# Hash attention and MLP mixer: both halves' scores of a head pair in a row, then both products with v

## The chip, the cores and the metric

One NeuronCore of a Trainium2 chip runs the whole program. The metric is device time in microseconds (us), the median of several executions. Runs of one kernel agree here to about 0.5%. Ratios are the mean time of one kernel's runs over that of the other's of the same rounds, so they are not quite the ratio of the medians.

## The reference, cut to what matters

```python
q_bits = (einsum('bhsd,dk->bhsk', q, proj) > 0)      # 6 hash bits per query, the same for keys
mask   = q_bucket[..., :, None] == k_bucket[..., None, :]
scores = where(mask, 0.125 * q @ k^T, -1e9)          # B=4, H=8, S=768, D=64
attn   = exp(scores - max) / sum
x      = (attn @ v) -> (B, S, 512)
u      = x + (relu(x^T @ w_tok1) @ w_tok2)^T          # then the channel MLP on u
```

The change touches attention only, the first 320 us of the program. Heads go in 16 pairs; a pair's 768 queries go in two halves of 384.

## The kernel before: the parts that matter

All arithmetic is fp32. Scores use two row groups of the TensorE array (64 rows each, one per head), the products with v two column groups (64 columns each), the sums of exponentials and the hash products four column groups of 32. The profile calls these forms 64\*128, 128\*64 and 128\*32. An fp32 matmul shows as two instructions (the 12 matmuls of one product with v as x24 in the lines below).

```python
def product(sc, t, c, start):                   # scores of chunk c (128 keys); bits matmul has t = bits
    for i in range(2):
        rows = slice(D * i, D * i + D)
        nc.tensor.matmul(sc[:, i, :HALF], t[rows, 1, P*c:P*c+P], t[rows, 0, qs], ...)
...
sc = psum.tile([P, 2, 512], F32, tag="sc", bufs=3)
product(sc, qkt, c, True); product(sc, bits, c, False)
e = pool.tile([P, 2, HALF], F32, tag="e", bufs=12)
nc.scalar.activation(e, sc[:, :, :HALF], ACT.Exp, scale=SCALE)
...
def hashes(n):                                  # bits of pair n: matmuls, then
    nc.vector.tensor_scalar(g, ps, 0.0, 0.5, op0=ALU.is_gt, op1=ALU.subtract)
    nc.scalar.mul(g, g, bitscale)
    ...                                         # eight small DMAs g -> bitrows, on the sync queue
def weigh(self):                                # the product with v, into ONE psum bank "acc"
    acc = psum.tile([P, 512], F32, name="acc", tag="acc", bufs=1)[:, :HALF]
    for c, e in enumerate(self.es):
        for i in range(2):
            nc.tensor.matmul(acc[D*i:D*i+D], vn[:, i, c], e[:, i], ...)
    nc.scalar.activation(nums[self.n][:, self.half], acc, ACT.Identity, scale=-1.0, bias=vsum)
...
for n in range(len(pairs)):                     # the loop, cut
    for half in range(2):
        now.scores()
        ...                                     # sums of the pair before, hashes(n + 1): if half == 0
        if before: before.weigh()               # product with v of the HALF before
        ...
        if half == 0: load_v(n + 1)
        before = now
```

So TensorE alternates: scores of one half, product of the half before, and so on.

In the lines below PE is TensorE, PEld its weight loads, DVE VectorE, ACT ScalarE, and SPq the sync engine's queue of DMAs. "num" is ACT's copy of a finished product out of PSUM, where this kernel's matmuls write. newton and divide make the reciprocals of the sums (rec, copied once by ACT) and multiply by them. join and turnover convert weights for the later stages, on VectorE with one square on ACT. A bounce, in every second pair, transposes two finished pairs on VectorE and sends them to DRAM in four DMAs.

## Time and profile before

| | before |
|---|---|
| time | 814.28 us, median of 3 |
| span of the profiled run | 811.9 us, of which attention to 321.69 |
| TensorE busy | 803.6 us (99%) |
| a pair of heads, on TensorE | 19.56 us |
| of it: two stretches of scores / two of products / sums / hash product | 10.09 / 8.04 / 0.67 / 0.76 us |

How to read it: with TensorE busy 99% of the span and the chain of waits made of matmuls, no other engine's share says what the kernel could gain.

### The profile page before, as it was taken

How to read it: one execution, taken by the hardware profiler on the slowest of the kernel's cores; microseconds unless marked ns; L12 is line 12 of the kernel's file. 1: busy time of each engine (PE TensorE's matmuls, PEld its weight loads, DVE VectorE, ACT ScalarE, POOL GpSimd, SP SyncE). 2: the span in 40 equal slices, each digit the busy share in tenths (PEclk: the TensorE clock that was granted, in tenths of full speed). 3: DMA queues.
4: the chain of work that ended last, by engine and by line, in shares of the span. 5: the costliest groups of instructions: out<-in, count | busy, mean ns of one | idle time of the engine just before them, and what ended most of it. 6: DMA issues, size and time to landing. Idle time of an engine off the chain costs nothing.

```text
span 811.9 us, 10567 instructions
## 1 busy us (share of the span) xinstructions
PE 803.6 (99%) x3901; PEld 471.6 (58%) x3901; DVE 664.1 (82%) x869; ACT 423.1 (52%) x675; POOL 42.5 (5%) x69
## 2 busy tenths in 40 slices
PE   9999999999999999999999999999999999999996
PEld 4444444444444444455544448876676886676885
DVE  4889898989898676899575969898669897778985
ACT  5787778788888776111022321236774335775111
POOL 1000000000000000000010110011010012000001
PEclk9999999999999999999999999999999999999999
DMA  4335353547444234562008894499854578730455
GB/s 161 128 137 171 132 174 130 159 133 231 140 130 119 81 81 139 173 214 97 1 0 300 297 349 156 176 274 252 272 136 142 210 231 194 232 118 1 160 178 110
DMA packets 88490, 132.30 MB, mean 163 GB/s; under 512 B 29480, under 2 KB 62704, under 8 KB 86128
## 3 DMA queue, kind: packets, MB, share of 16 engines
q1 hardware_dynamic: 82320, 112.60, 42.4%
q0 software_dynamic: 5552, 18.35, 9.4%
q8 instruction: 33, 0.54, 0.3%
q10 hardware_dynamic: 560, 0.61, 0.2%
q14 instruction: 25, 0.20, 0.1%
HBM read 97.21 MB, written 33.69 MB: 161 GB/s over the span
## 4 chain that ended last, share of the span: by engine, by line
PE 99%; DVE 0%; ACT 0%; issue 0%; ACTq 0%
PE b L709 49%; PE sc L345 20%; PE acc L392 16%; PE t L623 5%; PE t L642 5%; PE sums L416 2%; PE hp L306 1%; PE hw L324 1%; PE idle L454 0%; ACT vt L297 0%; ACT e L352 0%; ACT g L311 0%; DVE second L1128 0%; DVE g L310 0%; DVE bits L326 0%
## 5 line engine op out<-in xcount | busy, mean ns | idle before, releaser
L352 ACT ACTIVATE e<-sc 128x768 f32<-128x768 f32 x192 | 153.1, 811 | 13.4 <-PE sc L345 12.5
L345 PE MATMUL sc<-qk 64*128 64x384 f32 x768 | 158.5, 492 | 0.3 <-ACT e L352 0.3
L709 PE MATMUL b<-R,second 128*128 128x256 f32 (+1 forms) x612 | 150.9, 404 | 0.0
L715 ACT COPY c<-b 128x512 f32<-128x512 f32 (+1 forms) x78 | 37.4, 488 | 187.7 <-PE b L709 174.2
L709 PEld LDWEIGHTS b<-R,second 128*128 128x128 f32 x612 | 116.3, 190 | 31.6 <-issue 17.0
L392 PE MATMUL acc<-e,vn 128*64 128x384 f32 x768 | 130.9, 490 | 0.0
L384 DVE TENSOR_TENSOR esd<-esd,e 128x768 f32<-128x768 f32 x128 | 122.3, 955 | 10.4 <-ACT e L352 0.5
L345 PEld LDWEIGHTS sc<-qk 64*128 64x128 f32 x768 | 66.5, 187 | 55.8 <-issue 45.3
L392 PEld LDWEIGHTS acc<-e,vn 128*64 128x64 f32 x768 | 52.3, 137 | 74.9 <-issue 74.3
L709 PE MATMUL b<-XT,WC 128*128 128x256 f32 (+1 forms) x264 | 82.5, 456 | 0.0
L709 PEld LDWEIGHTS b<-XT,WC 128*128 128x128 f32 x264 | 50.2, 190 | 29.6 <-issue 25.1
L345 PE MATMUL sc<-bits 64*128 64x384 bf16 x384 | 62.9, 323 | 0.2 <-DVE bits L328 0.2
L623 PE MATMUL t<-x,W 128*128 128x512 f32 x96 | 41.8, 593 | 0.0
L642 PE MATMUL t<-W,r 128*128 128x384 f32 x128 | 41.8, 486 | 0.0
L398 ACT ACTIVATE num<-acc,vsum 128x384 f32<-128x384 f32 x32 | 18.6, 581 | 41.6 <-PE acc L392 41.2
L437 ACT COPY rec<-rec 32x384 f32<-32x384 f32 x64 | 32.6, 509 | 12.9 <-DVE rec L431 12.4
L380 DVE SCALAR_TENSOR_TENSOR esd<-e 128x768 f32<-128x768 f32 x32 | 30.5, 954 | 9.3 <-ACT e L352 9.3
L709 PE MATMUL b<-XT,SW 128*128 128x256 f32 (+1 forms) x120 | 34.6, 422 | 0.0
L642 PEld LDWEIGHTS t<-W,r 128*128 128x128 f32 x128 | 24.3, 190 | 17.6 <-issue 1.4
L345 PEld LDWEIGHTS <-bits 64*128 64x128 bf16 x384 | 19.3, 94 | 25.4 <-DVE bits L328 0.8
L709 PE MATMUL b<-TA,WC 128*128 128x512 f32 x72 | 33.8, 592 | 0.0
L709 PE MATMUL b<-TA,SW 128*128 128x512 f32 x72 | 32.9, 592 | 0.0
(176 smaller groups left out, 1052.7 us busy)
## 6 DMA issues: line engine op xcount, KB each, us to landing
second<-left SPq DMA_DIRECT2D x18, 1344.0 KB
raw<-in_moe_w_ch SPq DMA_DIRECT2D x16, 768.0 KB
qk<-in_qk SPq DMA_DIRECT2D x15, 768.0 KB
seen<-in_qk POOLq DMA_DIRECT2D x21, 384.0 KB, 4.2
WC<-hidden_left SPq DMA_DIRECT2D x15, 448.0 KB
vn<-in_v SPq DMA_DIRECT2D x16, 384.0 KB
vt<-in_vT SPq DMA_DIRECT2D x16, 384.0 KB
bounced<-stage SPq DMA_DIRECT2D x32, 192.0 KB
```

Of the source, the lines that this page charges most:

```text
L345: nc.tensor.matmul(sc[:, i, :HALF], t[rows, 1, P * c : P * c + P], t[rows, 0, qs], start=start, stop=not start,)
L352: nc.scalar.activation(e, sc[:, :, :HALF], ACT.Exp, scale=SCALE)
L380: nc.vector.scalar_tensor_tensor(self.d, es[0], NR * EPS, es[1], op0=ALU.add, op1=ALU.add,)
L384: nc.vector.tensor_tensor(self.d, self.d, e, op=ALU.add)
L392: nc.tensor.matmul(acc[D * i : D * i + D], vn[:, i, c], e[:, i], start=(c == 0), stop=(c == NR - 1),)
L398: nc.scalar.activation(nums[self.n][:, self.half], acc, ACT.Identity, scale=-1.0, bias=vsum,)
L416: nc.tensor.matmul(ps[at : at + 32], ones[:, :32], self.halves[h].d[:, i], start=True, stop=True,)
L437: nc.scalar.copy(rec[other : other + 32, h], rec[at : at + 32, h])
L623: nc.tensor.matmul(ps, W1[:, r, P * j : P * j + P], x[:, r], start=(r == 0), stop=(r == NR - 1),)
L642: nc.tensor.matmul(ps[:, :HALF], r1[:, j, P * cb : P * cb + P], W2[:, j, HALF * half : HALF * half + HALF], start=(j == 0), stop=(j == NJ ...
L709: nc.tensor.matmul(ps, left(k), right(k), start=start and k == ks[0], stop=stop and k == ks[-1], skip_group_check=True,)
L715: nc.scalar.copy(c, ps)
```

## The change

Intent: run the scores of both halves (12 chunks), then the sums of the pair before and the next pair's hash product, then both products with v. For this the second half's product takes one of the three score tiles as its accumulator, v is asked for a whole pair ahead, and the hash bits come before the last add of the exponentials' sum on VectorE. The core of the diff (cuts are marked):

```diff
             def weigh(self):
                 _, vn, _, vsum = loaded[self.n]
-                acc = psum.tile([P, 512], F32, name="acc", tag="acc", bufs=1)[:, :HALF]
+                if self.half:
+                    acc = psum.tile([P, 2, 512], F32, name="acc", tag="sc", bufs=3)[:, 0, :HALF]
+                else:
+                    acc = psum.tile([P, 512], F32, name="acc", tag="acc", bufs=1)[:, :HALF]
 ... (add split into add, four or five adds, and add_last; esd gets 4 buffers)
+            halves = [Half(n, half) for half in range(2)]
+            if n:
+                load_v(n + 1)
+            for now in halves:
                 now.scores()
+                now.add()
+                if now.half == 0:
+                    now.add_last()
+            if before:
+                before.sums()
+            if n + 1 < len(pairs):
+                hashes(n + 1)
+            halves[1].add_last()
+            if n == 0:
+                load_v(1)
+            load_qk(n + 2)
+            add_values(n)
+            if before:
+                before.newton()
+            weights.join()
+            halves[0].weigh()
 ... (the last pair is set apart)
+            if before:
+                before.divide()
+            weights.turnover()
+            halves[1].weigh()
+            if n and n % 2 == 0:
+                bounce(pool, n - 2)
 ... (the old loop over halves, all removed)
```

More of the change, by code (lines that the diff above doesn't have):

```diff
@@ L373, in scores, with add, add_last @@
                     first_hashes(0, 1)
-            def add(self, k):
+            def add(self):
                 es = self.es
-                if k == 0:
-                    self.d = pool.tile([P, 2, HALF], F32, name="esd", tag="esd", bufs=3)
-                    nc.vector.scalar_tensor_tensor(
-                        self.d, es[0], NR * EPS, es[1], op0=ALU.add, op1=ALU.add,
-                    )
-                for e in (es[2:4], es[4:])[k]:
+                self.d = pool.tile([P, 2, HALF], F32, name="esd", tag="esd", bufs=4)
+                nc.vector.scalar_tensor_tensor(
+                    self.d, es[0], NR * EPS, es[1], op0=ALU.add, op1=ALU.add,
+                )
+                for e in es[2:-1]:
                     nc.vector.tensor_tensor(self.d, self.d, e, op=ALU.add)
+            def add_last(self):
+                nc.vector.tensor_tensor(self.d, self.d, self.es[-1], op=ALU.add)
             def weigh(self):
                 _, vn, _, vsum = loaded[self.n]
-                acc = psum.tile([P, 512], F32, name="acc", tag="acc", bufs=1)[:, :HALF]
+                if self.half:
+                    acc = psum.tile([P, 2, 512], F32, name="acc", tag="sc", bufs=3)[:, 0, :HALF]
+                else:
+                    acc = psum.tile([P, 512], F32, name="acc", tag="acc", bufs=1)[:, :HALF]
                 for c, e in enumerate(self.es):
@@ L460, in attention @@
         )
-        before, both = None, []
+        before = None
         for n in range(len(pairs)):
-            for half in range(2):
-                now = Half(n, half)
+            halves = [Half(n, half) for half in range(2)]
+            if n:
+                load_v(n + 1)
+            for now in halves:
                 now.scores()
-                if half == n == 0:
-                    hashes(1)
-                if half == 0:
-                    add_values(n)
-                now.add(0)
-                quotients = None
-                if len(both) == 2:
-                    quotients, both = Quotients(both), []
-                    quotients.sums()
-                both.append(now)
-                if half == 0 and 0 < n < len(pairs) - 1:
-                    hashes(n + 1)
-                if half == 0:
-                    load_qk(n + 2)
-                if quotients:
-                    quotients.newton()
-                if half and n and n % 2 == 0:
-                    bounce(pool, n - 2)
-                now.add(1)
-                if half:
-                    weights.turnover()
-                else:
-                    weights.join()
-                if before:
-                    before.weigh()
-                if quotients:
-                    quotients.divide()
-                if half == 0:
-                    load_v(n + 1)
-                if half == 0 and n == 2 * NP:
-                    fetch(0, x0)
-                before = now
@@ L498, in attention @@
-        assert not (weights.fetched or weights.begun or weights.ready)
-        quotients = Quotients(both)
-        quotients.sums()
-        quotients.newton()
-        before.weigh()
-        quotients.divide()
+                now.add()
[8 more added lines that the diff above has]
+                load_v(1)
@@ new lines, in attention @@
+            load_qk(n + 2)
[4 more added lines that the diff above has]
+            halves[0].weigh()
+            if n + 1 == len(pairs):
+                before.divide()
+                before = Quotients(halves)
+                before.sums()
+                before.newton()
+                weights.turnover()
+                halves[1].weigh()
+                break
+            if before:
+                before.divide()
@@ L506, in careful_attention @@
+            weights.turnover()
+            halves[1].weigh()
+            if n and n % 2 == 0:
+                bounce(pool, n - 2)
+            if n == 2 * NP:
+                fetch(0, x0)
+            before = Quotients(halves)
+        assert not (weights.fetched or weights.begun or weights.ready)
+        before.divide()
     def careful_attention(pool, psum):
```

## The prediction

> **What bounds the kernel now.** I read the page first: the busy shares, the chain that ended last, and the slices.
>
> ```profile
> PE 803.6 (99%) x3901; PEld 471.6 (58%) x3901; DVE 664.1 (82%) x869; ACT 423.1 (52%) x675; POOL 42.5 (5%) x69
> ...
> PE 99%; DVE 0%; ACT 0%; issue 0%; ACTq 0%
> PE b L709 49%; PE sc L345 20%; PE acc L392 16%; PE t L623 5%; PE t L642 5%; PE sums L416 2%; PE hp L306 1%; PE hw L324 1%; PE idle L454 0%; ACT vt L297 0%; ACT e L352 0%; ACT g L311 0%; DVE second L1128 0%; DVE g L310 0%; DVE bits L326 0%
> ```
>
> The chain is matmuls nearly from end to end, so TensorE sets the time. The change touches only attention (sc, acc, sums, hp). No wait of another engine is on the path for it to take away: in the table of waits for attention PE waits 0.3 us for ACT and 0.2 us for DVE, once each, both in the first pair. What can still be gained lies inside PE's busy time, so I went to the order of time on PE, one stretch of scores and one of products with v (from 112.76 us):
>
> ```profile
> 112.76 0.92 PE L345 MATMUL sc<-qk 64*128 64x384 f32 x4
> 113.51 0.33 PE L345 MATMUL sc<-bits 64*128 64x384 bf16 x2
> 113.67 0.81 PE L345 MATMUL sc<-qk 64*128 64x384 f32 x4
> ...
> 116.90 0.81 PE L345 MATMUL sc<-qk 64*128 64x384 f32 x4
> 117.54 0.33 PE L345 MATMUL sc<-bits 64*128 64x384 bf16 x2
> 117.80 4.09 PE L392 MATMUL acc<-e,vn 128*64 128x384 f32 x24
> 121.82 0.92 PE L345 MATMUL sc<-qk 64*128 64x384 f32 x4
> ```
>
> Columns: start, duration, engine, line, what. A chunk of scores starts every 0.807 us ((116.90 - 113.67)/4), but the first takes 0.91 (112.76 to 113.67) and the last 0.90 (116.90 to 117.80): a stretch of six is 5.04 us where 6 x 0.807 = 4.84, so 0.20 lost. In the products, two narrower windows give starts of 118.82 for the last 18 instructions and 119.79 for the last 12: three pairs in 0.97, 0.323 a pair; 12 pairs would be 3.88, the stretch takes 4.02, so 0.14 to 0.15 lost (0.05 after its first pair, 0.10 at its end). One round of scores and products thus loses about 0.35 us at its two changes of form, rows 64*128 to columns 128*64 and back. A whole pair repeats every 19.56 us (121.82 - 102.26), 14 times from 24.02 to 297.86.
>
> Next, how much room DVE has, as its busy share in attention is the highest after PE's. Two neighbouring stretches start with the same instruction (L209):
>
> ```profile
> 103.82 0.95 DVE L209 SCALAR_TENSOR_TENSOR W<-raw,tmp 128x768 f32<-128x768 f32 x1
> ...
> 121.86 0.95 DVE L209 SCALAR_TENSOR_TENSOR WC<-raw,tmp 128x768 f32<-128x768 f32 x1
> ...
> 142.94 0.95 DVE L209 SCALAR_TENSOR_TENSOR WC<-raw,tmp 128x768 f32<-128x768 f32 x1
> ```
>
> The first round, without a bounce, is 18.04 us with 0.19 of marked waits: 17.85 of work. The second has the two transposes of a bounce (1.75) and 1.53 of waits: 19.55. Their mean, 18.7, is 96% of 19.56. DVE is a near second.
>
> Last, the hash bits: eight small transfers issued in order by one queue.
>
> ```profile
> 110.51 6.13 SPq L316 DMA_DIRECT2D bits<-g  x8
> ```
>
> They go out every 0.77 us. By the trace's records of landings, of those issued from 110.51 the first landed at 112.33, the fourth at 114.66 (4.15 after the first issue), the eighth at 117.74 (7.23 after). Before, they are needed from about 122.5: 4.8 us of slack for the eighth.
>
> [...] within one form the pace is even, and the loss of 0.35 us a round sits at the changes. [...] the trace has 955 for the adds. No cheaper add comes with this change. [...] 1.82 us from issue to landing for a 5.2 KB transfer. So making bits later does not shorten their way.
>
> **The change part by part.** No matmul, exponential, add, conversion or transfer is added or removed.
>
> (a) Both halves' scores in a row, both products in a row. Pairs 1 to 15 go from two rounds of scores and products to one: 15 x 0.35 = 5.3 us off PE. Pair 0 had its hash product between its two halves; now it comes after them: about 0.1 saved. The new period is 19.56 - 0.35 = 19.2 us. ACT follows: exponentials take 811 ns singly but run 6 in 4.40 us (0.73 each) when behind, at 309.38, faster than PE's 0.807, so twelve in a row build no backlog with three score tiles. The second half's acc takes a score tile, read by the 0.58 us copy to num; the ring is wanted again only with the third chunk, 1.6 us later. Hidden.
>
> (b) In pair 0, exponentials were held up by the hash and v sums on ACT, which cost PE 0.29 us of idle at 17.38 and about 0.1 of restart. That goes: 0.4. A 0.1 blip at 310.25 too.
>
> (c) v a whole pair ahead: the loads were never waited for. Zero.
>
> (d) Hash bits later. Counting from a pair's first score: scores end at 9.9, sums (0.67) and hash product (0.76) at 11.3. DVE starts its adds with the second exponential at 2.77 (24.02 to 26.79 in the trace), the first half's five take 5.12 (15.00 to 20.12), the next four 4.0: 11.9. Then g on DVE (0.56) and ACT (0.6): first issue about 13.2; fourth landed 17.4, eighth 20.4. The next pair starts at 19.2; its first bits product, 0.75 later at 19.95, needs the first four; the fourth chunk, at 22.4, needs the rest. Margins 2.5 and 2.0 us. After that DVE does the last add, newton 1.5, join 2.5, divide 0.9, about 0.3 of wait for ACT's square, turnover 2.5: ready at 21.0 (22.75 with a bounce), wanted at 19.2 + 2.77 = 21.97. So a bounce makes the next pair 0.8 late, and the one after catches up. The margins hold: no stall from pair 2 on.
>
> (e) Pair 0 to 1 is different. DVE writes the second half's query bits at 13.72, so adds start near 14.4; nine end at 23.5, bits made at 24.1, scaled at 24.7; the fourth transfer lands at 28.9, the eighth at 32.0. PE: scores end at 18.7 (13.61 + 5.05), hash 19.4, both products 27.3, first bits wanted 28.0. A stall of 0.9, and then of 0.7 at the fourth chunk (31.3): together 1.6 us, once.
>
> Sum: -5.3 - 0.1 - 0.5 + 1.6 = -4.3 us. The later stages (half the time) are untouched, and stay PE-bound.
>
> **Rivals.** (1) The bits matmul waits for all eight transfers instead of its own region. Then it waits until 20.4 against 19.95, up to 21.2 after a bounce: about 0.9 x 14 = 12 us lost, near 821. Against it: the eight writes go out every 0.77 us though each lands 1.82 us after its issue, so writes to disjoint parts are not ordered by the whole tile; reads probably neither. (2) DVE becomes the bound: 18.7 plus 0.3 of new wait is 19.0 of 19.2. If the change costs DVE 0.4 us more per pair, lateness grows 0.2 per pair, eats the 2.0 us margin in some ten pairs and then costs about 1 us: near 811. A larger backlog would give 814. (3) [...] say at the change of acc bank between the two products: 0.05 to 0.1 each, 1 to 1.5 us less gain, near 811.5. (4) No stall in pair 1, because bits come sooner than I order them: near 808.3.
>
> **Range and chances.** 814.28 - 4.3 = 810.0 us. The period's 0.35 is seen in every round, so I trust the gain to 1 us; the stalls can add several. The range that should hold it 8 times in 10 is 807.5 to 813.0. Faster by over 2% would need 16.3 us: all losses at changes in attention together are 32 x 0.35 = 11, so practically excluded (0.01). Slower by over 2% needs a stall of over 1.3 us in every pair (0.02). Within 2%: 0.97.
>
> **What would show it.** In the changed trace: a period of 19.2 us per pair on PE; 24 instructions of products directly followed by 24 more at 0.323 a pair; twelve chunks at 0.807 in a row; PE idle by DMA of 0.9 and 0.7 us at pair 1's bits and nowhere else; DVE's wait for the second exponential short or gone, alternating with the bounces; g on DVE about 12 us after a pair's first score. I would be wrong if PE waits for bits in every pair, if chunks of scores spread beyond 0.81 us (ACT as bound), or if the period doesn't shrink[...].

Cut from it, where marked, are statements about the hardware that no trace or run of this case shows; rival (3) is that the loss of 0.35 us moves instead of being saved. The adds took 955 ns (958 in the changed kernel), and the fourth of the eight transfers landed 4.15 us after the first issue (from 110.51; in the changed kernel 4.25, from 24.35).

## The result, and the profile after

809.07 us median of 4 (808.77 to 810.01) beside 813.57 for the kernel before on the same chip: ratio 0.9947, 95% interval 0.9929 to 0.9964. The gain is clear of noise and far inside 2%. Predicted was 810.0.

The page of the changed kernel, the lines that answer to those shown of before:

```profile
PE 798.4 (99%) x3901; PEld 475.0 (59%) x3901; DVE 662.0 (82%) x869; ACT 427.7 (53%) x675; POOL 42.6 (5%) x69
...
PE 97%; DVE 1%; SPq 1%; issue 0%; DMA 0%; ACT 0%; DVEq 0%; ACTq 0%
```

The counts of instructions in this row are the same, TensorE's busy time is 5.2 us less. New in the chain are 1% each of DVE and of the sync queue: it now passes through a wait of pair 1 that was not there. Pair 2 in order of time on TensorE (start, duration, engine, line, what):

```profile
47.61 0.92 PE L345 MATMUL sc<-qk 64*128 64x384 f32 x4
...
57.50 0.85 PE L421 MATMUL sums<-esd,ones 128*32 128x384 f32 x8
58.17 0.83 PE L306 MATMUL hp<-qk,projs 128*32 128x384 f32 x8
58.93 7.96 PE L397 MATMUL acc<-e,vn 128*64 128x384 f32 x48
66.82 0.92 PE L345 MATMUL sc<-qk 64*128 64x384 f32 x4
```

A pair takes 66.82 - 47.61 = 19.21 us. The twelve chunks take 9.89 (57.50 - 47.61) where two stretches of six took 5.04 and 5.05; the two products 7.89 (66.82 - 58.93) where they took 2 x 4.02; sums and hash product are as before. 0.20 and 0.15 us, the two losses of one round, are gone. This repeats to 0.01 us in pairs 2 to 14. Pair 1 is different:

```profile
27.02 0.92 PE L345 MATMUL sc<-qk 64*128 64x384 f32 x4
28.01 0.32 PE L345 MATMUL sc<-bits 64*128 64x384 bf16 x1
28.64 0.33 PE L345 MATMUL sc<-bits 64*128 64x384 bf16 x1 [0.32 <-DMA bits<-g]
...
31.57 0.33 PE L345 MATMUL sc<-bits 64*128 64x384 bf16 x1 [0.24 <-DMA bits<-g]
...
38.29 0.85 PE L421 MATMUL sums<-esd,ones 128*32 128x384 f32 x8
```

The stretch takes 11.27 us instead of 9.89: 1.38 us lost where the hash bits are waited for, in the first chunk and in the fourth. By the trace's records of landings the fourth of the eight transfers landed at 28.60 and the last at 31.52, just before the starts at 28.64 and 31.57. The marked waits (0.32 and 0.24) are less than the loss, because the ends of matmuls are modelled in the profile and part of a wait counts as busy; the distance between starts is what to trust.

Where the time went, by the starts of the two traces up to the first token matmul (321.69 before, 316.82 after, so 4.87 us): 14 periods x 0.351 = 4.91 gained; the last pair 0.46 (23.82 us before with three products, 19.49 after with two, a product being 12 x 0.3225 = 3.87); pair 0, from its first score to pair 1's, 0.57 (17.68 before with one product, 20.98 after with two); the first hash products started 0.30 earlier; less 1.38 in pair 1. The rest of the program took 490.2 us before and 490.3 after.

The 0.57 of pair 0 is not a change of form. The scores of its second half, before and then after:

```profile
14.39 0.92 PE L345 MATMUL sc<-qk 64*128 64x384 f32 x4
...
17.38 0.92 PE L345 MATMUL sc<-qk 64*128 64x384 f32 x4 [0.29 <-ACT e L352]
...
20.00 4.09 PE L392 MATMUL acc<-e,vn 128*64 128x384 f32 x24
```

```profile
13.30 0.92 PE L345 MATMUL sc<-qk 64*128 64x384 f32 x4
...
18.35 0.85 PE L306 MATMUL hp<-qk,projs 128*32 128x384 f32 x8
```

5.61 us became 5.05: a wait for ACT's exponentials is gone. The hash product takes 0.78 us in both places. In the last pair 0.1 of the 0.46 is such a wait too (at 310.25 before). So changes of form gained 5.3 us (15 rounds), spared waits for ACT about 0.7, and the stall in pair 1 took 1.38 back.

### The profile page after: what moved, and what is told of

Read it like the earlier page. It is cut to its first block, busy times and chain, and to the rows that moved or that the text cites. A ratio compares the mean times of both kernels' runs of the same rounds, so it can differ in the third digit from the quotient of the medians.

```text
span 807.1 us, 10537 instructions
## 1 busy us (share of the span) xinstructions
PE 798.4 (99%) x3901; PEld 475.0 (59%) x3901; DVE 662.0 (82%) x869; ACT 427.7 (53%) x675; POOL 42.6 (5%) x69
## 4 chain that ended last, share of the span: by engine, by line
PE 97%; DVE 1%; SPq 1%; issue 0%; DMA 0%; ACT 0%; DVEq 0%; ACTq 0%
PE b L715 50%; PE sc L345 19%; PE acc L397 15%; PE t L629 5%; PE t L648 5%; PE sums L421 2%; PE hp L306 1%; DVE esd L383 1%; SPq L316 1%; PE hw L324 0%; PE idle L459 0%; DMA bits<-g 0%; DVE esd L379 0%; DVE bits L326 0%; DVE esd L386 0%
## 5 line engine op out<-in xcount | busy, mean ns | idle before, releaser
L397 PE MATMUL acc<-e,vn 128*64 128x384 f32 x768 | 127.6, 488 | 0.0
L383 DVE TENSOR_TENSOR esd<-esd,e 128x768 f32<-128x768 f32 x96 | 92.0, 958 | 10.0
L715 PE MATMUL b<-TA,SW 128*128 128x512 f32 x72 | 32.9, 592 | 0.0
L756 POOL TENSOR_TENSOR c<-c 128x512 f32<-128x512 f32 x6 | 8.0, 1339 | 456.7 <-ACT c L721 435.2
```

Source lines behind the costliest of these rows:

```text
L383: nc.vector.tensor_tensor(self.d, self.d, e, op=ALU.add)
L397: nc.tensor.matmul(acc[D * i : D * i + D], vn[:, i, c], e[:, i], start=(c == 0), stop=(c == NR - 1),)
L715: nc.tensor.matmul(ps, left(k), right(k), start=start and k == ks[0], stop=stop and k == ks[-1], skip_group_check=True,)
```

## The experiments

All edits are against the changed kernel, and all ten kernels gave correct results. after_again, early_bits, sums_between and more_dve ran on one chip (kernel before: 813.56 us), the others on another (813.72 to 813.89). The last column is the ratio to the kernel before of the same rounds.

| run | what it tests | time us | ratio to before |
|---|---|---|---|
| after_again | yardstick | 809.06 | 0.9940 (0.9927 to 0.9953) |
| early_bits | pair 1's stall taken away | 807.85 | 0.9930 (0.9918 to 0.9943) |
| sums_between | two more changes of form a pair | 813.71 | 1.0012 (0.9997 to 1.0027) |
| more_dve | VectorE as second bound | 813.41 | 1.0002 (0.9987 to 1.0016) |
| extra32 | tiny product in another form | 814.46 | 1.0010 (0.9993 to 1.0027) |
| extra64 | the same in the same form | 811.20 | 0.9972 (0.9956 to 0.9989) |
| one_acc | the second accumulator taken away | 841.92 | 1.0336 (1.0316 to 1.0356) |
| v_late | v a pair later, at the queue's end | 817.91 | 1.0047 (1.0031 to 1.0064) |
| v_with_qk | v a pair later, behind qk | 809.83 | 0.9952 (0.9935 to 0.9969) |
| last_add_first | bits behind the last add | 810.24 | 0.9958 (0.9945 to 0.9972) |

The theory: the gain is the changes of form saved on TensorE, and nothing else in the change gains time by itself. The main rival: the new order spares TensorE waits for ACT, VectorE or v. The traces above already give the rival about 0.7 us, in the first pair and the last; the runs decide about the 0.35 us of every round.

**after_again** is the changed kernel unedited, for comparison.

> The changed kernel once more, on the chip of the next three, as their yardstick. 809 us, 0.994 to 0.996 of the kernel before; a period of 19.21 us a pair on TensorE and one stretch of scores of 11.27 us (pair 1) among stretches of 9.89.

It came out so.

**sums_between** gives the changes of form back with the same instructions and the same work on ACT and VectorE.

```diff
                 if now.half == 0:
                     now.add_last()
+                    if before:
+                        before.sums()      # the matmuls only
-            if before:
-                before.sums()
+            if before:
+                before.nearly()            # the two activations, where they were
```

> The matmuls of the sums stand between the two halves' scores, their ACT and VectorE work stays where it was: the same instructions, two more changes of form on TensorE a pair. Theory (a change of form costs about 0.1 us at the exit and 0.02 to 0.1 at the entry): 0.32 us more a pair, 15 pairs, 4.9 us more than the changed kernel, near 814, that is nearly all of its gain gone, with no idle of TensorE marked against ACT or VectorE. Rival (the gain came from waits of ACT or VectorE that the new order avoids): less than 1 us more.

813.71 us, 4.65 more than after_again. The sums, in pair 2 (the last bits matmul, the sums, the next half's scores):

```profile
52.79 0.33 PE L345 MATMUL sc<-bits 64*128 64x384 bf16 x2
53.05 0.85 PE L421 MATMUL sums<-esd,ones 128*32 128x384 f32 x8
53.83 0.92 PE L345 MATMUL sc<-qk 64*128 64x384 f32 x4
```

A bits pair is followed within a stretch after 0.16 us; here the sums start 0.26 after it, and the scores behind them 0.78 after instead of the 0.67 that hash products needed. Scores, sums and hash product of a pair take 11.66 us instead of 11.32: 0.34 for two changes, times 15 pairs 5.1. TensorE waits for ACT or VectorE nowhere in the pairs after the first. So the 0.35 us of a round lies in the order of TensorE alone.

**extra32 and extra64** do equal work, a tiny product of ones between the two products with v, and differ only in its form.

```diff
+            other = psum.tile([P, 512], F32, name="other", tag="sm", bufs=1)
+            nc.tensor.matmul(other[:32, :D], ones[:, :32], ones, start=True, stop=True)
             weights.turnover()
             halves[1].weigh()
```

extra64 has `other[:64, :D], ones[:, :64]`.

> The changed kernel with one tiny product of ones (64 columns wide as moving data, two instructions) between the two products with v of pairs 0 to 14, 32 columns of the array: another form than the products'. Theory (changes of form cost): two changes, so about 0.4 us a pair, 6 us in all[...]. Its partner, extra64, does the same work in the form of the products. Rival (any foreign matmul costs the same, form or not): both cost alike.

> As extra32, but with 64 columns of the array, the form of the products with v, so no change of form. Theory: its own 0.1 to 0.2 us a pair, 2 to 3 us in all, at least 0.2 us a pair less than extra32. Rival: the same as extra32.

extra32 first, then extra64, around the tiny product of pair 2:

```profile
62.89 0.30 PE L502 MATMUL other<-ones 128*32 128x64 f32 x2
63.12 4.09 PE L397 MATMUL acc<-e,vn 128*64 128x384 f32 x24
67.14 0.92 PE L345 MATMUL sc<-qk 64*128 64x384 f32 x4
```

```profile
62.53 0.22 PE L502 MATMUL other<-ones 128*64 128x64 f32 x1
62.53 0.54 PE L397 MATMUL acc<-e,vn 128*64 128x384 f32 x1
62.58 0.22 PE L502 MATMUL other<-ones 128*64 128x64 f32 x1
62.64 4.04 PE L397 MATMUL acc<-e,vn 128*64 128x384 f32 x23
66.61 0.92 PE L345 MATMUL sc<-qk 64*128 64x384 f32 x4
```

In another form the product stands alone between two stretches, each again 4.02 us long: the two take 8.27 instead of 7.89, 0.38 more. In the same form it slips in between (0.11 more a pair; the trace shows its two halves interleaved with those of the product). The difference, 0.27 us a pair or 4.0 in 15 pairs, shows as 3.3 us in the medians; pair 1's stall was also shorter in extra32, as its products ended later (10.89 against 11.15). Beside after_again the medians are 5.4 and 2.1 us higher (expected were 6, and 2 to 3). It is the change of form that costs, even between two forms that both use all 128 rows. What takes the time at a change was not shown; whether it is the weight load, which there starts only with its own matmul (last section), no run separates.

**early_bits** makes pair 1's bits after five adds on VectorE instead of nine.

```diff
                 now.scores()
+                if n == 0 and now.half == 1:
+                    hashes(1)
                 now.add()
 ...
-            if n + 1 < len(pairs):
+            if 0 < n < len(pairs) - 1:
                 hashes(n + 1)
```

> Only pair 0 differs: the hash bits of pair 1 are made after the first half's five adds on VectorE, not after nine. Theory (pair 1's loss is late bits, nothing else): bits issue near 20.4 instead of 24.35 us, the eighth lands near 27.6, in time, so pair 1's scores take 9.9 us instead of 11.27, and the time falls by 1.4 us against the changed kernel, to about 807.7. Rival (the first stretch is slow for another cause, such as first loads of v or the exponentials): pair 1 keeps over 11 us, the time stays at 809.

The queue of the bits and TensorE at pair 1:

```profile
20.45 6.09 SPq L316 DMA_DIRECT2D bits<-g  x8
```

```profile
26.91 0.92 PE L345 MATMUL sc<-qk 64*128 64x384 f32 x4
27.66 0.33 PE L345 MATMUL sc<-bits 64*128 64x384 bf16 x2
```

No wait is left, the stretch takes 9.89 us. The medians differ by 1.2 us (1.4 expected); the intervals of the two ratios overlap, so that the time alone would not prove it, but the trace does. It has the lowest median of all versions here.

**last_add_first** undoes the third part of the change.

```diff
                 now.add()
-                if now.half == 0:
-                    now.add_last()
+                now.add_last()
 ...
                 hashes(n + 1)
-            halves[1].add_last()
```

> The last add of the second half stands in front of the hash bits again. Theory: bits 0.9 us later in every pair; in pair 1 the first stall grows by 0.9 and the second stays, so its scores take about 12.2 us instead of 11.27; the eighth transfer of the later pairs still lands about 0.7 us or more before it is wanted, so no stall there; 0.9 us more than the changed kernel, near 810. Rival (the margin is smaller than worked out): stalls in many pairs, over 812.

810.24 us. Pair 1's stretch takes 12.33 us, 1.06 more; of the later ones only one is longer, by 0.08 us. So this part of the change is worth about 1 us, nearly all of it in pair 1.

**v_late** undoes the second part, or so I meant.

```diff
-            if n:
-                load_v(n + 1)
             for now in halves:
 ...
             if n == 2 * NP:
                 fetch(0, x0)
+            if n:
+                load_v(n + 1)
             before = Quotients(halves)
```

> v of the next pair is loaded at the end of a pair instead of a whole pair ahead. Theory (the loads were never waited for): within 0.3 us of the changed kernel, 809. Rival (fetching v a pair ahead is part of the gain): TensorE's products wait for a transfer, 1 us or more a pair, 820 or more.

A miss: 817.91 us. Below, the product with v of pair 9, and then a table of two stretches, in the wait and after it: length, busy time of PE, PEld, DVE, ACT and POOL (with counts), TensorE's granted clock (PEclk, 1.00 before the wait), the DMA engines' busy share and GB/s.

```profile
199.88 10.04 PE L397 MATMUL acc<-e,vn 128*64 128x384 f32 x48 [5.07 <-DMA vn<-in_v]
```

```profile
194.70:199.90 5.20, 0.13 (x6) 0.02 (x2) 5.03 (x9) 1.16 (x3) 0.00 (x0) 0.75 0.96 377
199.90:203.00 3.10, 3.10 (x10) 1.22 (x12) 1.18 (x2) 2.13 (x5) 0.00 (x0) 0.50 0.08 24
```

At n = 8 my edit had put v behind a bounce and the fetch of x0 (1.5 MB) in the one queue, and the DMA engines' share of 96% in the wait shows transfers still moving. The wait is 5.1 us, and then costs 2.1 more, as the clock had dropped to 0.50 during the wait (mean 0.75 in it, 0.50 after it) and the products took 9.97 us instead of 7.89. Smaller waits follow bounces in other pairs (0.33, 0.52 and twice 0.1 us). Together these are 8.3 us of the 8.8 that it lost against after_again. It does not say that v must come a pair ahead, so:

**v_with_qk** puts v right behind the hash bits and qk, as before the change.

```diff
-            if n:
-                load_v(n + 1)
             for now in halves:
 ...
-            if n == 0:
-                load_v(1)
             load_qk(n + 2)
+            load_v(n + 1)
```

> After the miss of v_late. v of the next pair is issued right behind the hash bits and qk, as in the kernel before, so not a whole pair ahead but ahead of the bounce and of the fetch of x0 in the same queue. Theory (v_late lost its time because v stood behind the x0 fetch and the bounces, not because v was loaded within one pair): no stretch of sums and hash product is longer than 1.45 us, no wait for v, 809 us as the changed kernel. Rival (in the new order v must be a whole pair ahead wherever it stands): waits for v again, over 812.

809.83 us, a ratio of 0.9952 where the changed kernel has 0.9947: no wait for v, all stretches as in the changed kernel. v a whole pair ahead gains nothing that the right place in the queue doesn't.

**one_acc** takes the second accumulator away.

```diff
-                if self.half:
+                if False:
                     acc = psum.tile([P, 2, 512], F32, name="acc", tag="sc", bufs=3)[:, 0, :HALF]
```

> Both products with v use the one acc bank, as before the change; the second half no longer takes a score tile. In the changed kernel the copy of the first half's product to num ends 17.15 us after the pair's first score, and the first product ends at 15.27. Theory (the second bank is what hides ACT's lateness): the second product waits about 1.9 us for that copy and restarts in 0.1, in 14 pairs and the last: about 2.0 x 15 = 30 us more, near 839, slower than before by 3%. Rival (products do not wait for num): no change.

841.92 us, the largest effect of all. The two products of a pair:

```profile
64.91 4.09 PE L397 MATMUL acc<-e,vn 128*64 128x384 f32 x24
70.80 4.09 PE L397 MATMUL acc<-e,vn 128*64 128x384 f32 x24 [1.79 <-ACT num L403]
```

The second waits 1.79 us for the copy of the first to leave the bank, since ACT is then still at the reciprocals, and the pair's products take 9.90 us instead of 7.89. Beside after_again the run takes 32.9 us more (30 expected): without the second tile the new order loses seven times what it gains. Pair 0 lost most in one place:

```profile
26.66 5.79 PE L397 MATMUL acc<-e,vn 128*64 128x384 f32 x24 [2.59 <-ACT num L403]
```

After this wait of 2.59 us TensorE's granted clock was 0.50 from 27.6 to 30.9 us, and the product took 5.71 us (to 32.37) instead of 4.02. After the wait of 1.79 us in pair 2 the clock stayed at 1.00 (66.00 to 75.00 us).

**more_dve** adds one VectorE operation a pair.

```diff
             halves[1].add_last()
+            nc.vector.tensor_tensor(halves[1].d, halves[1].d, halves[1].d, op=ALU.max)
```

> One more VectorE operation per pair (the maximum of the half's sum with itself, 128x768, about 0.95 us, changes no value), right after the last add. VectorE's measured idle in the changed kernel is 0.93 us in two pairs, 0.46 a pair. Theory (VectorE is a near second bound): it gets about 0.5 us later in each pair while weights are converted (pairs 1 to 11), the margin of the hash bits of 2 us is used up after about four, and then TensorE follows VectorE: 3 to 4 us more than the changed kernel, near 812.5. Rival (VectorE has room, as it has 18% idle over the kernel): no more than 0.5 us.

813.41 us, 4.35 more: VectorE is the near second bound. But the way there is not the expected one. TensorE and then ACT at the first stall, pair 6 (124.81 is its first score):

```profile
127.64 0.92 PE L345 MATMUL sc<-qk 64*128 64x384 f32 x4 [0.95 <-ACT num L403]
```

```profile
125.75 0.58 ACT L403 ACTIVATE num<-acc,vsum 128x384 f32<-128x384 f32 x1
126.23 0.90 ACT L208 ACTIVATE raw<-raw 128x768 f32<-128x768 f32 x1
127.02 0.57 ACT L403 ACTIVATE num<-acc,vsum 128x384 f32<-128x384 f32 x1
```

VectorE's reciprocals come late, ACT's copies of them wait, and in ACT's order both num copies stand behind these. The second num frees the score tile that the product had borrowed, and the third chunk of the next pair waits for it. In the changed kernel that copy ends 19.91 us after a pair's first score and the third chunk wants the tile at about 20.9: a margin of 1.0 us. ACT idles another 1.33 us before that copy (pair 2, waiting for the product), so the reciprocals may come about 2.3 us later. That is no less than what the bits have: after pair 1 their last transfer lands 1.5 to 2.2 us before it is wanted, by the records of landings and the pace of the chunks.

So the two margins run out together. The added operation stands behind the bits and before the reciprocals in VectorE's order, so it delays the reciprocals once more. The tile marks three of the four stalls (0.95, 0.67 and 0.56 us), the bits the one in pair 10 (0.22 us). In pair 6 the last transfer landed at 128.35, by my estimate 0.4 us later than the fourth chunk would have wanted it; the stall at the tile hides this.

## Why the prediction was right, by its own steps

- **(a) Changes of form.** Predicted 0.35 us a pair and a period of 19.2; measured 0.351 and 19.21. sums_between and the pair extra32/extra64 show the cause: the same instructions with two more changes cost 0.34 us a pair, and a foreign form costs 0.27 more than a like one. The twelve chunks in a row kept 0.807, so ACT did not become the bound.
- **The score tile for the second product** was called hidden. It is, but one_acc shows that it carries the change, and more_dve that it is one of two margins that a later VectorE uses up.
- **(b) Pair 0 and the blip.** Predicted 0.1 + 0.4 + 0.1; measured 0.57 in pair 0, and 0.46 in the last pair, which is 0.35 and the blip of 0.1. That the sum is right is luck: the hash product's new place saved nothing (0.78 us in both), and the wait for ACT with its restart cost 0.56 and not 0.4.
- **(c) v ahead: zero.** Right for the change, as v_with_qk shows. My test of it in v_late failed by its own fault, the place in the queue.
- **(d) No stall from pair 2 on.** Right: bits go out 13.18 us after the pair's first score in pair 2 (predicted 13.2). The lateness after a bounce was over-estimated: 0.8 predicted, 0.4 measured, because the wait of 0.3 us for ACT's square that I had put into VectorE's round is not there (the lines below: bounce, late add, and the next pair with a wait left).

```profile
68.24 1.83 DVE L241 STREAM_TRANSPOSE stage<-XT 128x768 f32<-128x768 f32 x2
69.99 0.92 DVE L379 SCALAR_TENSOR_TENSOR esd<-e 128x768 f32<-128x768 f32 x1
...
88.79 0.96 DVE L379 SCALAR_TENSOR_TENSOR esd<-e 128x768 f32<-128x768 f32 x1 [0.93 <-ACT e L352]
```

  The add at 69.99 is 3.17 us after the pair's first score (66.82), the one at 88.79 is 2.76 after its own (86.03) and waited 0.93: VectorE's slack is 0.93 us in two pairs.
- **(e) Pair 1.** Predicted stalls of 0.9 and 0.7, 1.6 in all, measured about 0.8 and 0.6 by the starts, 1.38 in all; early_bits shows that late bits are all of it. The term was 0.2 us too large.
- **The rivals.** (1) fell: no pair but the first after the start waits for bits, and there the matmul started at 28.64, with the fourth transfer landed and four still to come, so it waits for its own part. (2) did not happen; where more_dve brings it about, the loss comes first by ACT's copy and the score tile, a route that the prediction did not see, and in one stall of four by bits. (3) fell: 48 instructions of products run at an even pace through the change of bank (24 pairs x 0.3225 = 7.74 of the stretch's 7.89 us, the same 0.15 lost as in one product before). (4) fell with (e), and early_bits brings it about.
- **The sum.** -4.3 predicted, -4.5 in the medians, -4.87 in the traces, of which I count 0.30 at the start as no part of the change: the first hash products of the same code took between 1.75 and 2.86 us in the profiled runs.

## What to carry to other kernels

Where one engine is busy 99% of the time, look at the distance between the starts of its instructions and for where that is longer than the steady pace; here each change of TensorE's form was worth 0.1 to 0.2 us, and an order with two fewer a pair gained 5.3 us in the trace, 4.5 us net, without removing a matmul. Before lengthening stretches, look for the tile that must be free, the queue place of each load and the first round, where nothing is ahead yet: the first decided between a gain and a loss of 3%, the last gave back a quarter of the gain.

## What the traces show of form changes, weight loads, the clock and waits

- What a change of form takes, for 384-column fp32 matmuls, by the starts in the changed kernel's pair 2: about 0.10 us at the exit from a form, and at the entry 0.02 (128\*32), 0.05 (128\*64) or 0.1 us (64\*128) more, so 0.35 us for scores to products and back; extra32 and extra64 put two changes between like stretches at 0.27 us.
- In the products with v, which use all 128 rows, each weight load starts with the matmuls of the pair before it, 0.32 us ahead of its own. At the changes of form of pair 2 (57.50, 58.92 and 66.82) it does not, and the profile marks no other engine as the cause ("issue" at all three). The weight loads at the end of pair 2's products and at pair 3's first scores:

```profile
66.07 0.14 PEld L397 LDWEIGHTS acc<-e,vn 128*64 128x64 f32 x2 [0.18 <-issue]
66.81 0.30 PEld L345 LDWEIGHTS sc<-qk 64*128 64x128 f32 x4 [0.60 <-issue]
```

  The first serves the last products, started at 66.39; the second begins with its own matmul at 66.82. The first four of these matmuls last 0.92 us, later fours 0.81; whether the load makes that difference, no run tests.
- The granted clock fell in two of the waits. In v_late it was 1.00 from 194.8 to 197.2 us and 0.50 from 197.4 on, some 2.5 us into the wait of 5.1 (mean over the wait 0.75). In one_acc a wait of 2.59 us was followed by 0.50 (27.6 to 30.9 us; mean over 1.00 to 32.00 us 0.94); one of 1.79 us was not.
- The marks show only a part of a wait behind a matmul, whose end the profile models: the marked waits in pair 1 were 0.56 us where the starts show 1.38 lost.
